# Hedgehog linear attention beside a gated MLP: query features turned by VectorE in 32-by-32 blocks instead of by TensorE, and the side work set from a table

## The chip, the cores and the metric

One core of one Trainium2 chip. The metric is the device time of one execution in microseconds: the median of the runs shown. The profile is one execution of the same program, with the hardware profiler on. PE is TensorE's matmul part and PEld its weight load, DVE is VectorE, ACT is ScalarE, POOL is GpSimd, SP is SyncE, which issues most DMAs.

## The reference

`x` is 2048 tokens by 640. It is normalised per token (`xn`), and two branches read it:

```python
qkv = (xn @ wqkv) -> q, k, v          # 32 heads of 20
pq = einsum("bhsd,hdf->bhsf", q, w_phi); pk = the same of k
phi_q = concat([softmax(pq), softmax(-pq)]); phi_k = the same of pk   # 40 features a head
kv = einsum("bhsf,bhsd->bhfd", phi_k, v);  z = sum of phi_k over s
num = phi_q @ kv;  den = phi_q @ z + 1e-6
s = (num / den) @ wo
g = silu(gelu(xn @ w1 + b1) @ w2 + b2)      # 640 -> 1536 -> 640
out = x + s * g
```

## The kernel before

All products are of 32-bit numbers. The large ones are split in a high and a low part (`split_w`, lines 134 to 140; hi by ScalarE, the rest by VectorE or GpSimd) and take three passes (`PASSES`, line 337).

**Phase 1** (0 to 238 us) projects keys, values and queries tile by tile of 128 tokens, sums the key-value state in PSUM, and stores the exponentials of each query tile, 128 tokens by 1280 features, in `e_dram`. The change does not touch it.

**The feed-forward units** (238 to 552 us) are 12: two halves of the tokens (1024 each, as two groups of 512), six groups of 256 hidden columns. A unit is seven groups of products (`part`, L1201, 54 products of 512 columns) and a down pass in two halves of 30 products (`down`, L1230), which VectorE adds to `ys` (L1239). Beside it run, called by hand at chosen points of the unit: loading and splitting `w1` and `w2`; and for each of 16 query tiles `q_load` (read back from `e_dram`) and `q_norm` (L1286 to L1305): GpSimd multiplies with the key sums (L1288), VectorE sums heads twice (L397), takes reciprocals (L1291, L1299) and three small products (L1295, L1298, L1301), GpSimd scales (L402), and SyncE stores the tile, token by token, in `phi_dram` (L1273).

**The tail** (from the last down pass on) works on four chunks of 512 tokens. A chunk's four tiles of `phi` are loaded. The products with `kv` need features on the partitions, so TensorE turns them: `num_t` (L1318 to L1328) makes four 128-by-120 transposes into a bank of PSUM (L1324) and ScalarE copies the bank to `ph` (L1327); 11 such steps per chunk. `num_m` then multiplies `ph` with the state `bdk` (120 features by 64 columns, L1335, 256 tokens at a time) or, for the last two heads, `bdl` (L1342); a 32-bit product shows as two instructions in the trace. ScalarE and VectorE split the result into `oT` (L1338, L1339) and `oTl` (L1347, L1348), and a DMA that ScalarE issues spreads rows of `oTl` into `oT` (`spread`). `finish` makes one output tile (five per chunk) of 15 products with `wo` (L1402), multiplies with the gate (L1404, two halves), adds the residual (L1405) and stores.

In `last_mid` and `num_groups`, the turning and the products of chunk 0 stand between the down products of the last unit, and those of the next chunk between the output tiles of the present one.

The order on each engine is the order in which the code emits instructions (`manual_schedule`); SyncE's queue too stands in that order. Tiles of SBUF come from pools (23 `slabs` of 5 KB a partition, 11 `rows`), PSUM has 8 banks in this part, and a new tile waits for the last reader of the one it replaces.

Of the kernel before, what the change touches and what calls it, by code (L numbers as in the profile page):

```python
# [40 lines left out]
def _ft(t):  # L41
    return (120 * t, 120 if t < 10 else 80)


@with_exitstack
def hedgehog_gated_mlp_kernel(ctx: ExitStack, tc: tile.TileContext, x, xt_in, wqk, bd, wv, wo, w1, b1, w2, b2, out_t):
# [47 lines left out]
    phi_dram = dram.tile([NT, P, 2 * D], F32, name="phi_dram")  # L94
# [491 lines left out]
    def w1_forms(raws):  # L586
# [632 lines left out]

    ys = [None] * KC  # L1220

    def down(g, ws, hs, o, mid=None):
        for ds in ((0, 1, 2), (3,), (4,)):
            pss = [bankB() for _ in ds]
            for i in range(GF):
                for d, ps in zip(ds, pss):
# [5 lines left out]
            for d, ps in zip(ds, pss):  # L1232
                if ys[d] is None:
                    ys[d] = slab(F32, f"y{d}", (P, 2, CW))
                y = ys[d][:, o, :]
                if g == 0:
                    nc.vector.tensor_copy(y, ps[:])
                else:
                    nc.vector.tensor_tensor(y, ps[:], y, op=OP.add)  # L1239
# [8 lines left out]
    def x_back(p):  # L1248
        hi, lo = slab(F32, "xhi", (P, 10, P)), slab(F32, "xlo", (P, 10, P))
        nc.sync.dma_start(hi[:], xp_dram[:, :, 0, at(p)])  # L1250
        nc.sync.dma_start(lo[:], xp_dram[:, :, 1, at(p)])
        return hi, lo

    def x_forms(p, hi, lo):
        nc.vector.tensor_tensor(hi[:], hi[:], lo[:], op=OP.add)
        yield
        tt = lo[:, :9]
        x_sums(lambda a, b: hi[:, a:b], lambda a, b: hi[:, a + 8:b + 8] if b <= 2 else hi[:, a + 3:b + 3], tt)
        yield
# [4 lines left out]
        nc.sync.dma_start(xd_dram[:, :, 1, at(p)], tt)


    stores, late_store = [], [False]

    def put(dst, src):
        if late_store[0]:  # L1270
            stores.append((dst, src))
        else:
            nc.sync.dma_start(dst, src)  # L1273

    def put_old(n):
        for _ in range(n):
            nc.sync.dma_start(*stores.pop(0))

    def q_load(t):
# [3 lines left out]
        return ef  # L1283

    def q_norm(t, ef):
        ez = slab(F32, "ez")  # L1286
        zv = ez[:].rearrange("p a b -> p (a b)")
        nc.gpsimd.tensor_tensor(zv, ef, zf, op=OP.mult)  # L1288
        yield
        rc = head_sums(ef, "rc")  # L1290
        nc.vector.reciprocal(rc[:], rc[:])  # L1291
# [26 lines left out]
    def num_t(phi, p, j):  # L1318
        ps = bankB()
        n = 120 if j < 5 else 80  # L1320
        for e in range(2):
            f, q = (2 * j + e, p) if j < 5 else (10, e)
            for i in range(2):
                nc.tensor.transpose(ps[:n, e * 256 + i * P:e * 256 + (i + 1) * P].bitcast(F32R),  # L1324
                                    phi[2 * q + i][:, 120 * f:120 * f + n], identr[:])
        ph = (row if (2 * j + p) % 2 else ph_tile)([P, 512], F32, "ph")
        nc.scalar.activation(ph[:n], ps[:n], AF.Copy)  # L1327
# [327 lines left out]
```

## Time and profile before

| | us |
|---|---|
| runs | 661.45, 661.48, 662.12; median 661.48 |
| profiled execution, its span | 659.8 |
| TensorE busy | 652.2 (99%), granted clock 1.00 |
| VectorE, ScalarE, GpSimd busy | 449.2, 325.4, 392.8 |
| DMA | 130.62 MB, mean 198 GB/s |
| transposes by TensorE (L1324), 176 | 542.6 to 626.1 |

The profile gives the span of its execution, from the first to the last instruction; it is 1.6 us under the median of the runs, which holds what lies around the span. A row of a group ends in busy time, mean ns of one, and idle time ahead of it with its releaser. A row of the chain is start, length and what.

### The profile page before, as it was taken

Reading aid. Unit: us, or ns where it says so; the run is one execution under the profiler, and the core shown is the slowest. Engines: PE = TensorE matmul, PEld = TensorE weight load, DVE = VectorE, ACT = ScalarE, POOL = GpSimd, SP = SyncE. Lnnn points to the kernel's source line nnn. Section 1 sums busy time; section 2 is a strip of 40 time slices with the busy share of each in tenths; the row PEclk is TensorE's granted clock in tenths of the full one; section 3 lists DMA queues with packets and bytes.
Section 4 is the critical chain, followed back from the end, with each engine's and each line's share of the span. In section 5 each row is a group of like instructions: output and inputs, shape, how many; then the busy total and the mean of one; then the engine's idle time right before and its main releaser. Section 6 shows DMA issues by size and latency. Waiting matters only on the chain.

```text
span 659.8 us, 11974 instructions
## 1 busy us (share of the span) xinstructions
PE 652.2 (99%) x4616; PEld 572.6 (87%) x4616; DVE 449.2 (68%) x714; ACT 325.4 (49%) x550; POOL 392.8 (60%) x344
## 2 busy tenths in 40 slices
PE   8999999999999999999999999999999999999997
PEld 8999999999999998888888888888888887877876
DVE  5878987766885756595885685777967877333132
ACT  4556777644666678435245138632132336645320
POOL 3597887774883437776875754746357665422322
PEclk9999999999999999999999999999999999999999
DMA  8436912031924882539656697456375275668444
GB/s 319 184 121 205 294 63 67 27 102 37 299 87 147 312 310 81 198 118 321 222 178 246 249 425 290 167 223 243 120 283 199 81 307 230 209 215 316 139 133 148
DMA packets 77081, 130.62 MB, mean 198 GB/s; under 512 B 5056, under 2 KB 44480, under 8 KB 76128
## 3 DMA queue, kind: packets, MB, share of 16 engines
q1 hardware_dynamic: 76704, 129.20, 55.0%
q10 hardware_dynamic: 320, 0.66, 0.6%
q8 instruction: 36, 0.59, 0.3%
q14 instruction: 21, 0.17, 0.1%
HBM read 81.66 MB, written 46.20 MB: 194 GB/s over the span
## 4 chain that ended last, share of the span: by engine, by line
PE 94%; POOL 2%; DMA 1%; issue 1%; DVE 1%; ACT 0%; SPq 0%; POOLq 0%
PE pB L1230 25%; PE pB L1201 22%; PE pW L485 20%; PE pB L1402 10%; PE pA L344 4%; PE pW L977 3%; PE pB L1335 3%; PE pB L1324 2%; PE pA L163 2%; PE kv L577 1%; DMA folds<-in_wqk_dram 1%; POOL tt L276 1%; POOL xd L295 0%; PE pB L1342 0%; PE pA L330 0%
## 5 line engine op out<-in xcount | busy, mean ns | idle before, releaser
L1230 PE MATMUL pB<-hs,w2s 128*128 128x512 f32 x720 | 167.0, 390 | 0.0
L1230 PEld LDWEIGHTS pB<-hs,w2s 128*128 128x128 f32 x720 | 134.6, 188 | 28.2 <-DVE oT L1339 0.4
L1201 PE MATMUL pB<-xp,w1s 128*128 128x512 f32 x324 | 81.3, 389 | 0.0
L1201 PE MATMUL pB<-xd,w1s 128*128 128x512 f32 x324 | 79.3, 389 | 0.0
L1239 DVE TENSOR_TENSOR y<-pB,y 128x512 f32<-128x512 f32 x100 | 63.7, 680 | 15.8 <-PE pB L1230 15.6
L1402 PE MATMUL pB<-oT,wo 128*128 128x512 f32 (+1 forms) x315 | 72.5, 385 | 0.2
L1201 PEld LDWEIGHTS pB<-xd,w1s 128*128 128x128 f32 x324 | 60.8, 188 | 12.6
L1201 PEld LDWEIGHTS pB<-xp,w1s 128*128 128x128 f32 x324 | 60.8, 188 | 12.6
L1206 ACT ACTIVATE pB<-pB,b1t 128x512 f32<-128x512 f32 x48 | 31.8, 662 | 77.6 <-DVE pB L1497 28.3
L1402 PEld LDWEIGHTS pB<-oT,wo 128*128 128x128 f32 x315 | 56.1, 188 | 13.0 <-DVE oT L1339 1.2
L402 POOL TENSOR_TENSOR eq<-eq,rc 128x1280 f32<-128x1280 f32 x16 | 37.9, 2369 | 48.7 <-DVE rc L1301 43.8
L383 POOL TENSOR_TENSOR e<-e,mxs 128x1280 f32<-128x1280 f32 x13 | 30.7, 2372 | 41.4 <-DVE mxs L378 25.7
L389 ACT ACTIVATE e<-e 128x1280 f32<-128x1280 f32 x32 | 40.8, 1274 | 17.9 <-POOL e L383 8.3
L601 POOL TENSOR_TENSOR w1s<-raw,w1s 128x640 fp32r<-128x640 f32 (+1 forms) x18 | 24.9, 1386 | 41.2 <-ACT w1s L600 41.1
L485 PE MATMUL pW<-wsum,xd 128*128 128x320 f32 x288 | 48.4, 310 | 0.0
L1288 POOL TENSOR_TENSOR ez<-eq,zrep 128x1280 f32<-128x1280 f32 x16 | 47.3, 2954 | 0.0
L1217 ACT ACTIVATE x<-pB 128x512 f32<-128x512 f32 x12 | 7.2, 600 | 78.9 <-PE pB L1201 78.9
L485 PEld LDWEIGHTS pW<-wsum,xd 128*128 128x128 f32 x288 | 43.6, 188 | 0.0
L138 POOL TENSOR_TENSOR w2s<-raw,w2s 128x640 fp32r<-128x640 f32 x24 | 37.1, 1567 | 7.1 <-ACT w2s L136 7.1
L402 POOL TENSOR_TENSOR e<-e,rc 128x1280 f32<-128x1280 f32 x15 | 36.1, 2410 | 5.8 <-DVE rc L838 4.2
L1327 ACT ACTIVATE ph<-pB 120x512 f32<-120x512 f32 (+1 forms) x44 | 22.9, 604 | 26.5 <-PE pB L1324 23.8
L1212 DVE TENSOR_TENSOR hs<-pB,hs 128x512 fp32r<-128x512 f32 x48 | 32.0, 685 | 5.2 <-ACT hs L1208 5.0
(216 smaller groups left out, 1282.1 us busy)
## 6 DMA issues: line engine op xcount, KB each, us to landing
raw<-in_w_dram SPq DMA_DIRECT2D x42, 320.0 KB
e_dram<-e SPq DMA_DIRECT2D x16, 640.0 KB
eq<-e_dram SPq DMA_DIRECT2D x16, 640.0 KB
phi_dram<-eq SPq DMA_DIRECT2D x16, 640.0 KB
phi<-phi_dram SPq DMA_DIRECT2D x16, 640.0 KB
xt<-in_x_dram SPq DMA_DIRECT2D x16, 320.0 KB
xres<-in_xt_dram SPq DMA_DIRECT2D x20, 256.0 KB
out_dram<-xres SPq DMA_DIRECT2D x18, 256.0 KB
```

The lines of the kernel that those rows point to most:

```text
L138: eng.tensor_tensor(sl[:, 1, :], raw, sl[:, 0, :].bitcast(F32), op=OP.subtract)
L383: eng.tensor_tensor(e3, e3, mx[:, :, None].to_broadcast([P, 64, DH]), op=OP.subtract)
L389: nc.scalar.activation(ef, ef, AF.Exp)
L402: eng.tensor_tensor(e3, e3, rc[:, :, None].to_broadcast([P, 64, DH]), op=OP.mult)
L485: nc.tensor.matmul(self.bank[ch][:, :HALF], self.x(blk, a), w(b), start=new and i == 0, stop=i == len(mms) - 1, skip_group_check=True)
L1201: nc.tensor.matmul(bank[ch][:], tl[:, a, off + wo_:off + wo_ + P], mov(blk, b), start=new and n == 0, stop=n == len(mms) - 1, skip_group_c ...
L1206: nc.scalar.activation(ps, ps, AF.Gelu_apprx_tanh, bias=b1t[:, f:f + 1])
L1212: nc.vector.tensor_tensor(hs[:, 1], ps, hs[:, 0].bitcast(F32), op=OP.subtract)
L1230: nc.tensor.matmul(ps[:], ws[i][:, b, d * P:(d + 1) * P], hs[o][i][:, a, :], start=i == n == 0, stop=(i, n) == (GF - 1, 2), skip_group_che ...
L1239: nc.vector.tensor_tensor(y, ps[:], y, op=OP.add)
L1288: nc.gpsimd.tensor_tensor(zv, ef, zf, op=OP.mult)
L1402: nc.tensor.matmul(ps[:, cols], w, o[:, a, cols], start=n == 0, stop=n == 14)
```

## The change

**The turning.** After scaling, VectorE turns each query tile in 32-by-32 blocks, in two halves of 640 features (`q_turn`), into a tile `pt` that holds two token tiles side by side. Four DMAs for each half of a pair, one per 32 partitions, store it feature by feature (`q_put2`): `phi_dram` is now by chunk, 1280 features by 512 tokens, and each run is 64 tokens (256 bytes). For the products, 120 features by 512 tokens (twice) or the last 80 are read straight into `ph`. `num_t`, its transposes and ScalarE's copies are gone. `num_m` multiplies 512 tokens at a time; the split to `oT` puts the tokens back in order (`by_token`).

**The table.** All side work of this part is set by numbers. `tick` counts places: 31 in each unit, then two in each output tile (one ahead of it, one after eight of its products); `when(place, f)` puts a step there. 372 is the place ahead of the first output tile.

```diff
+PLAN = {
+    "q": [
...
+        [351.75, 371.75, 372.55, 372.75, 373.75, 373.85, 374.75, 376.1],
+        [367.0, 374.25, 375.3, 375.5, 376.0, 376.6, 377.5, 377.6, 381.5, 378.6],
+        [370.25, 377.75, 378.55, 378.75, 379.75, 379.85, 380.75, 380.85],
+        [377, 381, 381.8, 382.5, 383, 383.1, 384, 384.1, 385, 385.1],
+    ],
...
+    "c_q": ["pool", "pool", "pool", "pool", "vector", "pool", "pool", "pool", "pool", "pool", "vector", "pool", "pool", "pool", "pool", "pool"],
...
-    phi_dram = dram.tile([NT, P, 2 * D], F32, name="phi_dram")
+    phi_dram = dram.tile([NCH, 2 * D, CW], F32, name="phi_dram")
...
+    def when(s, f, *args):
+        assert int(s) >= at_slot[0]
+        e = todo.setdefault(int(s), [])
+        e.append((s % 1, len(e), f, args))
+
+    def tick():
+        for _, _, f, args in sorted(todo.pop(at_slot[0], ()), key=lambda e: e[:2]):
+            f(*args)
+        at_slot[0] += 1
...
-        scale_heads(ef, rc)
-        yield
-        put(phi_dram[t], ef)
...
+    def q_scale(t):
+        scale_heads(qe[t][0], qe[t][2], ENG[PLAN["c_q"][t]])
+
+    def q_turn(t, h):
+        c, (u, v) = t // TPC, divmod(t % TPC, 2)
+        if v == 0:
+            pairs[c, u, h] = slab(F32, "pt", (P, 20, 2, 32))
+        nc.vector.transpose(pairs[c, u, h][:, :, v, :],
+                            qe[t][0][:, D * h:D * h + D].rearrange("p (b k) -> p b k", k=32))
+        if h:
+            qe.pop(t)
+
+    def q_put2(t, h):
+        c, u = t // TPC, t % TPC // 2
+        pt = pairs.pop((c, u, h))
+        dst = phi_dram[c, D * h:D * h + D].rearrange("(b i) n -> i b n", i=32)
+        for a in range(4):
+            nc.sync.dma_start(dst[:, :, P * a + 64 * u:P * a + 64 * u + 64],
+                              pt[32 * a:32 * a + 32].rearrange("p b t k -> p b (t k)"))
...
+    def load_phi_group(c, j):
+        if j == 5:
+            t = tail_row([P, CW], F32, "ph")
+            nc.sync.dma_start(t[:80], phi_dram[c, 1200:])
+        else:
+            t = slab(F32, "ph", (P, 2, CW))
+            nc.sync.dma_start(t[:120], phi_dram[c, 240 * j:240 * j + 240].rearrange("(e p) n -> p e n", p=120))
...
-            for i in range(2):
-                nc.tensor.transpose(ps[:n, e * 256 + i * P:e * 256 + (i + 1) * P].bitcast(F32R),
-                                    phi[2 * q + i][:, 120 * f:120 * f + n], identr[:])
-        ph = (row if (2 * j + p) % 2 else ph_tile)([P, 512], F32, "ph")
-        nc.scalar.activation(ph[:n], ps[:n], AF.Copy)
...
-                nc.tensor.matmul(po[64 * e:64 * e + 64, :256], bdk[:n, 2 * j + e, :], ph[:n, e * 256:(e + 1) * 256],
+                nc.tensor.matmul(po[64 * e:64 * e + 64, :], bdk[:120, 2 * j + e, :], ph[:120, e, :],
                                  start=True, stop=True)
...
+    def num_step(c):
...
+        j = nsteps[c].pop(0)
+        num_m(j, oTs[c], phis[c].pop(j))
+        if j < 5:
+            spread(j, oTs[c])
...
                 for n, (w, o, a) in enumerate(steps):
+                    if n == 8 and sl.start == 0:
+                        tick()
                     nc.tensor.matmul(ps[:, cols], w, o[:, a, cols], start=n == 0, stop=n == 14)
...
-            put(out_t[d * P:(d + 1) * P, c * CW:(c + 1) * CW], xr[:])
+            when(at_slot[0] + 2, nc.sync.dma_start, out_t[d * P:(d + 1) * P, c * CW:(c + 1) * CW], xr[:])
```

The eight numbers of a row of `q` are the places of load, product with the key sums, first head sum, second head sum, the four small steps, scaling and the two turns of one tile; a row of an odd tile ends with the places of the two stores. `c_q` names the engine that scales.

TensorE in the tail. Before, from the second half of the last unit's down pass (L1230) to the third output tile (L1402):

```order
L1230 MATMUL pB<-hs,w2s 128x512 x12
L1342 MATMUL pB<-ph,bdl 40x256 x2
L1335 MATMUL pB<-ph,bdk 64x256 x20
L1230 MATMUL pB<-hs,w2s 128x512 x12
L1402 MATMUL pB<-oT,wo 128x512 x15
L1324 MATMUL pB<-identr,phi 80x128 x4
L1324 MATMUL pB<-identr,phi 120x128 x12
L1402 MATMUL pB<-oT,wo 128x512 x15
L1324 MATMUL pB<-identr,phi 120x128 x16
L1402 MATMUL pB<-oT,wo 128x512 x15
```

And now (L1322 the down pass, L1459 and L1451 the feature products, L1519 the output tiles):

```order
L1459 MATMUL pB<-ph,bdl 40x256 x2
L1322 MATMUL pB<-hs,w2s 128x512 x3
L1451 MATMUL pB<-ph,bdk 64x512 x2
L1322 MATMUL pB<-hs,w2s 128x512 x3
L1451 MATMUL pB<-ph,bdk 64x512 x2
L1322 MATMUL pB<-hs,w2s 128x512 x12
L1451 MATMUL pB<-ph,bdk 64x512 x6
L1322 MATMUL pB<-hs,w2s 128x512 x12
L1519 MATMUL pB<-oT,wo 128x512 x8
L1459 MATMUL pB<-ph,bdl 40x256 x2
L1519 MATMUL pB<-oT,wo 128x512 x7
L1451 MATMUL pB<-ph,bdk 64x512 x2
```

The transposes are gone, and the feature products stand singly, between smaller groups of the others.

VectorE in the tail. Before, from the last addition of the down pass on (the second head sum and the small steps of the last query tile, then output tiles):

```order
L1239 TENSOR_TENSOR y_4736<-pB,y_4736 128x512
L397 TENSOR_REDUCE dn<-ez 128x64
L1295 TENSOR_TENSOR dn<-dn,rc 128x64
L1298 SCALAR_TENSOR_TENSOR den<-dn 128x32
L1299 RECIPROCAL den<-den 128x32
L1301 TENSOR_TENSOR rc<-rc,den 128x64
L1404 TENSOR_TENSOR y_4684<-pB,y_4684 128x256 x2
L1404 TENSOR_TENSOR y_4692<-pB,y_4692 128x256 x2
```

And now, from the fourth output tile on, with the turns of tile 14 and the sums of tile 15:

```order
L1521 TENSOR_TENSOR y_4760<-pB,y_4760 128x256 x2
L1409 STREAM_TRANSPOSE pt<-eq 128x20x32 x2
L475 TENSOR_REDUCE rc<-eq 128x64
L1386 RECIPROCAL rc<-rc 128x64
L1521 TENSOR_TENSOR y_4784<-pB,y_4784 128x256 x2
L475 TENSOR_REDUCE dn<-ez 128x64
L1394 TENSOR_TENSOR dn<-dn,rc 128x64
L1397 SCALAR_TENSOR_TENSOR den<-dn 128x32
L1398 RECIPROCAL den<-den 128x32
L1400 TENSOR_TENSOR rc<-rc,den 128x64
```

The norms of tiles 12 to 15 moved from the last two units to behind the last down addition, between the output tiles.

SyncE in the tail, from the stores of tile 13 to the loads of chunk 3. Now:

```order
L1419 DMA phi_dram<-pt 32x20x64 x4
L1492 DMA xres<-in_xt_dram 128x512
L1308 DMA out_dram<-xres 128x512 x2
L1492 DMA xres<-in_xt_dram 128x512
L1419 DMA phi_dram<-pt 32x20x64 x8
L1492 DMA xres<-in_xt_dram 128x512
L1308 DMA out_dram<-xres 128x512
L1435 DMA ph<-phi_dram 80x512
L1438 DMA ph<-phi_dram 120x2x512 x2
```

Before, the last stores of features and what followed:

```order
L1380 DMA xres<-in_xt_dram 128x512 x2
L1273 DMA phi_dram<-eq 128x1280 x2
L1380 DMA xres<-in_xt_dram 128x512
L1312 DMA phi<-phi_dram 128x1280 x2
L1380 DMA xres<-in_xt_dram 128x512
```

Two stores of whole tiles became sixteen of half pairs, and the last eight stand six output tiles later, right ahead of the loads that read them.

More of the change, by code (lines that the diff above doesn't have):

```diff
@@ L1263, in x_forms @@
         nc.sync.dma_start(xd_dram[:, :, 0, at(p)], hi[:, :9])
[L1264 to L1277, printed above, removed]
+        nc.sync.dma_start(xd_dram[:, :, 1, at(p)], lo[:, :9])
+        seen.add(("x", p))
+    qe = {}
@@ L1350, in spread @@
+                hi, lo = (by_token(oT[1][:40, b])[:, 2 * e:2 * e + 2] for b in range(2))
+                nc.scalar.activation(hi, src, AF.Copy)
+                nc.vector.tensor_tensor(lo, src, hi.bitcast(F32), op=OP.subtract)
     def spread(j, oT):
         nc.scalar.dma_start(oT[0][j][15::16].bitcast(F32), oT[1][8 * j:8 * j + 8].bitcast(F32))
[L1353 to L1367 removed]
+    def num_step(c):
+        if c not in oTs:
+            oTs[c] = new_oT(slabs if PLAN["c_oT"][c] == "slab" else late[0])
+            nsteps[c] = [5, 0, 1, 2, 3, 4]
+        j = nsteps[c].pop(0)
+        num_m(j, oTs[c], phis[c].pop(j))
+        if j < 5:
+            spread(j, oTs[c])
@@ L1513, in hedgehog_gated_mlp_kernel @@
                 q_sub(eb[o], 2 + o, nc.gpsimd)
-        next(xo, None)
-        silu(3)
-        hs = ((h11, h21), (None, h22))
-        if unit == NG - 1:
-            reload()
-        if unit == 0:
-            zf = kv_norm(kvr_out[0])
-        if not more:
-            phin = load_phi(ORDER[1])
+            zf_at.append(kv_norm(kvr_out[0]))
+        tick()
+        if last:
+            done[0] = True
+            seen.difference_update({("y", g, o, d) for o in range(2) for d in range(KC)})
@@ L1523, in hedgehog_gated_mlp_kernel @@
             xstack.close()
             ctx.enter_context(tc.tile_pool(name="pad", bufs=1)).tile([P, 32], F32, name="lpad")
-            late = ctx.enter_context(tc.tile_pool(name="late", bufs=10, reuse_waits="tile"))
-            tailp.append(ctx.enter_context(tc.tile_pool(name="phs", bufs=6)))
+            late.append(ctx.enter_context(tc.tile_pool(name="late", bufs=11, reuse_waits="tile")))
+            tailp.append(ctx.enter_context(tc.tile_pool(name="phs", bufs=3)))
             tailp.append(ctx.enter_context(tc.tile_pool(name="gts", bufs=3)))
-        w1f = w1_forms(w1r) if more and not back else none
@@ L1529, in hedgehog_gated_mlp_kernel @@
-        if back:
-            w1g = w1_back((unit + 1) % NG)
-        next(w1f, None)
-        if not more:
-            oT = new_oT(late)
-            groups = last_mid()
-        dn = down(g, w2g, hs, 0, None if more else delayed(groups, 4))
-        next(dn)
-        h12 = act_lo(*h12)
-        if unit == 0:
-            for o in range(2):
-                q_put(eb[o], 14 + o)
-        next(q1, None)
-        next(w1f, None)
-        next(dn)
-        next(w1f, None)
-        next(dn)
-        if not more:
-            next(dn)
-            next(dn)
-            break
@@ L1571, in hedgehog_gated_mlp_kernel @@
-        next(dn)
-        next(xg, None)
-        next(q2, None)
+        tick()
+        w2g = [w2_at.pop((unit, i)) for i in range(GF)]
+        hs = ((h11, h21), (None, h22))
+        for d, _ in enumerate(down(g, w2g, hs, 0)):
+            if d == 0:
+                h12 = act_lo(*h12)
+                if unit == 0:
+                    for o in range(2):
+                        q_put(eb[o], 14 + o)
+            if d == 3 and unit == NG:
+                kv_state(kvr_out[0])
+        hs = (None, (h12, h22))
@@ L1605, in hedgehog_gated_mlp_kernel @@
+            finish(c, d, oTs[c], ci == NCH - 1 and d >= 3)
+    for _ in range(3):
+        tick()
+    assert not todo
     ffn.close()
```

369 lines of the change are left out of this document (203 added, 166 removed), and 12 rows, old and new, of the table PLAN.

## The prediction

> **What bounds the kernel now.** First the page: busy times, the granted clock, and the chain of work that ended last.
>
> ```profile
> span 659.8 us, 11974 instructions
> PE 652.2 (99%) x4616; PEld 572.6 (87%) x4616; DVE 449.2 (68%) x714; ACT 325.4 (49%) x550; POOL 392.8 (60%) x344
> PEclk9999999999999999999999999999999999999999
> PE 94%; POOL 2%; DMA 1%; issue 1%; DVE 1%; ACT 0%; SPq 0%; POOLq 0%
> PE pB L1230 25%; PE pB L1201 22%; PE pW L485 20%; PE pB L1402 10%; PE pA L344 4%; PE pW L977 3%; PE pB L1335 3%; PE pB L1324 2%; PE pA L163 2%; PE kv L577 1%; DMA folds<-in_wqk_dram 1%; POOL tt L276 1%; POOL xd L295 0%; PE pB L1342 0%; PE pA L330 0%
> ```
>
> TensorE is busy 99% of the span at the full clock, and 94% of the chain is its work. A microsecond taken off TensorE is a microsecond of span as long as nothing else becomes late. So two questions: how much TensorE work goes, and what is late then.
>
> Next the chain in order of time, around the tail (start us, us, what):
>
> ```profile
> 537.50 5.44 PE pB L1230 x24
> 542.94 0.24 PE pB L1324 x4
> ...
> 544.62 1.26 PE pB L1324 x16
> ...
> 546.65 1.25 PE pB L1324 x16
> ...
> 548.67 0.61 PE pB L1324 x8
> ```
>
> and from the same view 12 us later:
>
> ```profile
> 552.10 0.56 PE pB L1342 x4
> 552.66 4.32 PE pB L1335 x40
> ...
> 558.62 0.40 DVE y L1239
> 559.02 1.96 DMA oT<-oTl
> 560.99 0.74 ACT wo L136
> ...
> 561.79 1.58 POOL wo L138
> ...
> 564.15 1.20 PE pB L1324 x16
> 565.35 3.52 PE pB L1402 x15
> 568.87 1.26 PE pB L1324 x16
> ...
> 573.64 0.93 PE pB L1324 x12
> ```
>
> L1324 is the turning by TensorE: 44 transposes per chunk of 512 tokens, always on the chain. Between 558.62 and 563.41 the chain leaves TensorE: a small lapse before the first output product. Last, how full the engines are by stretch; the columns are length, then busy time (instructions) of PE, PEld, DVE, ACT, POOL, then clock, DMA share, GB/s:
>
> ```profile
> 499.40:525.30 25.90, 25.90 (x116) 21.45 (x115) 20.27 (x32) 9.15 (x15) 21.50 (x14) 1.00 0.39 147
> 565.30:590.00 24.70, 24.70 (x150) 19.25 (x150) 7.30 (x20) 12.46 (x28) 8.65 (x11) 1.00 0.73 253
> 590.00:616.00 26.00, 26.00 (x168) 20.57 (x167) 8.07 (x23) 10.96 (x25) 7.14 (x10) 1.00 0.72 240
> ```
>
> The first row is a feed-forward unit: TensorE has no gap in it, and VectorE some 5 us of 26 free. In the tail VectorE has 17 of 25 free.
>
> **The turning goes.** Chunk 0: 0.24 + 1.26 + 1.25 + 0.61 = 3.36 us. Chunk 1: 1.20 + 1.26 + 0.93 = 3.39 us. Chunks 2 and 3 have the same 44 instructions and the same counts; at 3.39 each the sum is 13.5 us, the 2% that the chain gives L1324. All 176 lie on the chain, so 13.5 us leave it. The 44 copies out of PSUM on ScalarE (L1327) go too; ScalarE is half idle, and that is worth nothing by itself.
>
> **The feature products** (L1335) become 80 instructions of 512 columns instead of 160 of 256. Now 40 take 4.32 us, 108 ns each, so two take 216 ns. A 512-column product of the down pass takes 5.44 / 24 = 227 ns. So the cost is 80 x (0 to 11 ns) = 0 to +0.9 us; I take +0.4.
>
> **The lapse.** From 552.10 to 564.15 are 12.05 us. In it TensorE's own work is 0.56 + 4.32, then 12 down products (12 x 0.227 = 2.72) and the 15 products of the first output tile (3.52): 11.12. So 0.9 us is lost there. In the changed order the feature products of chunk 0 stand one by one between the down products, and each tile of weights `wo` is split before: I take all 0.9 off, with 0 as the other end.
>
> Dense, that gives 13.5 + 0.9 - 0.4 = 14.0 us less.
>
> **What becomes late: the last four query tiles.** Before, tiles 14 and 15 had their sums while the last unit ran. Now tiles 12 to 15 are normalised, turned and stored in the tail, after the last down pass. Chunk 3 is made of just these four, and TensorE stands in order: the first product of chunk 3 (the 40-column one after the eight products of output tile 10) blocks everything behind it. I work out when TensorE gets there and when the data does. The rows (mean ns of one is the last figure before the second bar):
>
> ```profile
> L1288 POOL TENSOR_TENSOR ez<-eq,zrep 128x1280 f32<-128x1280 f32 x16 | 47.3, 2954 | 0.0
> L402 POOL TENSOR_TENSOR eq<-eq,rc 128x1280 f32<-128x1280 f32 x16 | 37.9, 2369 | 48.7 <-DVE rc L1301 43.8 <-issue 4.9
> L397 DVE TENSOR_REDUCE rc<-eq 128x64 f32<-128x1280 f32 x16 | 23.6, 1476 | 0.0
> L1291 DVE RECIPROCAL rc<-rc 128x64 f32<-128x64 f32 x16 | 8.9, 553 | 0.6
> L1295 DVE TENSOR_TENSOR dn<-dn,rc 128x64 f32<-128x64 f32 x16 | 8.8, 551 | 0.0
> L1298 DVE SCALAR_TENSOR_TENSOR den<-dn 128x32 f32<-128x32 f32 x16 | 7.3, 459 | 0.5
> L1299 DVE RECIPROCAL den<-den 128x32 f32<-128x32 f32 x16 | 5.7, 353 | 0.5
> L1301 DVE TENSOR_TENSOR rc<-rc,den 128x64 f32<-128x64 f32 x16 | 3.6, 225 | 0.6
> L1237 DVE COPY y<-pB 128x512 f32<-128x512 f32 x20 | 13.2, 685 | 5.1 <-PE pB L1230 5.1
> L1348 DVE TENSOR_TENSOR oTl<-pB,oTl 40x256 fp32r<-40x256 f32 x8 | 3.4, 421 | 2.6 <-ACT oTl L1347 2.6
> ```
>
> The trace has no 32-by-32 transpose. It reads and writes 640 numbers a partition; the copy of 512 takes 0.685 us and the reduction of 1280 takes 1.476. Between these ends I take 0.78, as 640 is nearer to 512. Two more rows of the timeline show that instructions back to back cost less than their means:
>
> ```profile
> 522.74 1.82 DVE L1239 TENSOR_TENSOR y<-pB,y 128x512 f32<-128x512 f32 x3
> ...
> 641.93 0.76 DVE L1404 TENSOR_TENSOR gt<-pB,gt 128x256 f32<-128x256 f32 x2 [2.64 <-issue]
> ```
>
> So 0.61 us for a 512-column one, 0.76 for the two halves of an output tile. VectorE's queue from the last down addition to the second turn of tile 15, counted in the order: 8 reductions (11.8), 4 reciprocals (2.2), 4 times the four small steps (4 x 1.59 = 6.4), 8 turns (6.2), 4 `oTl` parts (1.7), 7 `oT` parts (4.3), 6 output tiles (4.6): 37.2 us. TensorE in that time, from the end of the down pass T: 158 output products at 3.52 / 15 = 0.235 (37.1) and the features of chunks 1 and 2 (2 x 4.88 = 9.8): it arrives at T + 46.9.
>
> After the turns comes the store. Its row, the nearest there is, is a store of 512-byte packets:
>
> ```profile
> DMA packets 2083, 1.05 MB, mean 175 GB/s; under 512 B 32, under 2 KB 2083, under 8 KB 2083
> q1 hardware_dynamic: 2083, 1.05, 58.0%
> xd_dram<-xlo SPq DMA_DIRECT2D x1, 576.0 KB
> ```
>
> That answer is for 310 to 316 us: 0.58 x 6 us x 16 engines / 2083 = 26.7 ns a packet of 512 bytes. The new store has packets of 256 bytes, 2560 for a half tile pair, 160 an engine: at half a packet's time 2.1 us, at the whole 4.3; I take 3.2 (20 ns). With some 2 us to land (the `oT` row above, 1.96), 0.4 to issue each way, and the load of 160 KB and its landing (2.5), chunk 3 is ready 8.5 us after the turns: T + 0.7 + 37.2 + 8.5 = T + 46.4, if VectorE never waits. That is just in time. But it does wait. The scaling by GpSimd (2.37) needs the four small steps, and the turn right behind needs the scaling; between them stand one output tile and an `oT` part (0.76 + 0.61). So about 1.0 us is lost per tile, 4 us in all, and the arrival of chunk 3 is at T + 50.4: a new stall of 3.5 us. Its ends are 0 and, with the longer turn (8 x 0.7 = 5.6) and the longer packet (1.1), 10.
>
> Forecast: the profiled span 659.8 - 14.0 + 3.5 = 649.3. The median of the runs, 661.5, lies 1.7 above that span, so 651.0.
>
> **Other edits with one answer.** In the units the side work is now set at 31 places per unit, one query tile a unit: VectorE gets 2 turns (1.6 us) where the row above has 5 us free, and loses the second tile of the late units (two reductions, a reciprocal and the four steps, 5.1 us). Low parts moved between GpSimd and VectorE lie beside TensorE. SyncE now waits for a turn ahead of each store, and the loads of weights queue behind it. In the table they stand 10 places (of 25.9 / 31 = 0.84 us) or more ahead of their use, and the wait is short, since the store stands behind its turn: nothing. In the tail, residuals, gates and `ph` queue behind the store of tile 15; all are for output tile 10 and later, so what they cost is in the sum. Even before, SyncE stood 13 us at a store in the tail, and nothing came late:
>
> ```profile
> 554.20 12.98 SPq L1273 DMA_DIRECT2D phi_dram<-eq  x2
> ```
>
> **A rule against the change.** The row gives 26.7 ns for a 512-byte store packet; nothing in this trace stores less. The Trainium skill, DMA: Bandwidth & Descriptors, Specifications, says that line rate needs at least 512 B, and that below this the engine does a read-modify-write. By that rule 256 bytes would cost no less than 512, and a read added to the write could double it. With the whole packet time of the row (4.3 instead of 3.2 us) the sum is 652.1; what double would do is worked out as the third rival.
>
> **Rivals.**
>
> *No new stall.* VectorE's small steps (0.55 and 0.46 on average, 0.2 for the like-sized last one) may be quick when GpSimd is idle; that is 4 x 0.6 = 2.4 us less, and with packets at half the row's time 1.1 less: T + 46.9, in time. 661.5 - 14.0 = 647.5. Chance 0.22.
>
> *VectorE becomes the bound of the tail.* If it falls back, PSUM banks come free late and TensorE also waits in chunk 2's features; stalls of 7 to 12 us, 654.5 to 659.5. For it: 37.2 us of VectorE work in 47. Chance 0.16.
>
> *Slower: the stores.* The stores of tiles 13 and 15 are 640 packets an engine, starting near T + 21, with 8 us of other transfers among them. At p ns a packet they end at T + 29 + 0.64p, and 4 us later the data is there. The whole gain is gone when the stall is 14, at T + 61: p = 44 ns. At twice the row, 53 ns, it is T + 67, a stall of 20 and 667.5 us. Against it: the 512-byte stores of the row move 175 / 0.58 = 302 GB/s, and the tail at 565 to 590, with rows of 2 KB and more, 253 / 0.73 = 347, so shorter packets have so far cost 15%. Chance 0.12. (The rule of the Trainium skill above would lead here, and no run yet shows it.)
>
> *It does nothing measurable*, the stalls eating all but 1.3 us: 0.04.
>
> **The numbers.** The forecast, stalls of 1.5 to 6.5 us (649 to 654), has 0.46. The range 646.5 to 659.0 holds it, the dense case and nearly all of the third: some 0.83. A measurement here tells 0.2%, 1.3 us, from no change. Faster 0.84, same 0.04, slower 0.12.
>
> **What would show it.** Right: no transposes on TensorE; in the tail TensorE idle once, 2 to 6 us, ahead of chunk 3's first product, released by the load of `ph`; VectorE busy over 34 of the 47 us after the last down pass; turns of 0.7 to 0.85 us; store packets of 13 to 27 ns. Wrong: gaps between units 1 and 11; turns over 1 us; stalls at chunk 2; packets over 40 ns.

## The result and the profile after

The changed kernel takes 667.49 us (median of 4 runs, 666.20 to 668.42); the kernel before, beside it on the same chip, 661.77. The ratio is 1.0088, with a 95% interval of 1.0073 to 1.0102: slower, where 651.0 was forecast, and above the top of the range (659.0).

The page of the changed kernel, busy times and chain:

```profile
span 666.4 us, 11468 instructions
PE 647.2 (97%) x4360; PEld 550.6 (83%) x4360; DVE 468.2 (70%) x731; ACT 304.0 (46%) x488; POOL 387.5 (58%) x339
PEclk9999999999999999999999999999999999999799
PE 77%; DMA 7%; POOL 5%; DVE 4%; ACT 3%; issue 2%; SPq 1%; ACTq 0%; POOLq 0%; DVEq 0%
```

TensorE works 5 us less than before (652.2), but the span is 6.6 us longer. A quarter of the chain is now outside TensorE, where it was 6%, and in one slice near the end the granted clock is down. What TensorE waited for, of the list of waits (us in total, times, longest):

```profile
PE pB L1519 <- DMA oT<-oTl: 8.4, 6, 4.3
PE pB L1459 <- DMA ph<-phi_dram: 1.4, 1, 1.4
...
PE pB L1280 <- POOL w1s L679: 0.9, 1, 0.9
```

The stall that the prediction was about, the wait of chunk 3's first product for `ph`, is there with 1.4 us. The big one stands above it: the output products (L1519) wait six times for the spread, the small DMA that puts rows of `oTl` into `oT`. To see where the 6.6 us lie, one needs the starts of units 0, 2 and 11, and of the output products. Before (timeline of TensorE; below it the row of the output products: count, ns of one, first and last start):

```profile
238.25 1.55 PE L1201 MATMUL pB<-xp,w1s 128*128 128x512 f32 x6
...
292.15 1.52 PE L1201 MATMUL pB<-xp,w1s 128*128 128x512 f32 x6
...
525.10 1.52 PE L1201 MATMUL pB<-xp,w1s 128*128 128x512 f32 x6
L1402 PE MATMUL pB<-oT,wo x315: 278/389/504, 559.8 to 655.3; 128*128 128x512 f32 x143, 128*128 128x256 f32 x15
```

and after:

```profile
239.02 1.55 PE L1280 MATMUL pB<-xp,w1s 128*128 128x512 f32 x6
...
295.19 1.52 PE L1280 MATMUL pB<-xp,w1s 128*128 128x512 f32 x6
...
528.27 1.52 PE L1280 MATMUL pB<-xp,w1s 128*128 128x512 f32 x6
L1519 PE MATMUL pB<-oT,wo x315: 278/389/765, 560.3 to 662.2; 128*128 128x512 f32 x143, 128*128 128x256 f32 x15
```

| stretch | before | after | difference |
|---|---|---|---|
| up to unit 0 | 238.25 | 239.02 | +0.8 |
| units 0 and 1 | 53.90 | 56.17 | +2.3 |
| units 2 to 10 | 232.95 | 233.08 | +0.1 |
| unit 11 to the first output product (turning and features of chunk 0 in it) | 34.7 | 32.0 | -2.7 |
| first to last output product (chunks 1 to 3 in it) | 95.5 | 101.9 | +6.4 |
| rest | 4.5 | 4.2 | -0.3 |

The first row differs as much between executions of one and the same code (237.8 to 239.0 in the runs below) and is not pursued. So three things are to be explained: 2.3 us in units 0 and 1, and a tail that is 6.4 us longer although 10.2 us of turning (three chunks at 3.39) have left it.

The tail, after, in the timeline of TensorE: chunk 2's last features, then output tile 10, where chunk 3's first features stand.

```profile
605.52 1.08 PE L1451 MATMUL pB<-ph,bdk 120*64 120x512 f32 x4
606.53 8.95 PE L1519 MATMUL pB<-oT,wo 128*128 128x512 f32 x38
616.85 0.63 PE L1459 MATMUL pB<-ph,bdl 80*40 80x256 f32 x4 [1.37 <-DMA ph<-phi_dram]
...
622.95 1.62 PE L1519 MATMUL pB<-oT,wo 128*128 128x512 f32 x3 [4.34 <-DMA oT<-oTl]
624.49 1.98 PE L1451 MATMUL pB<-ph,bdk 120*64 120x512 f32 x4
```

The spread of chunk 2 lands 4.34 us late. And the four feature products behind it take 1.98 us instead of 1.08: the clock. Two-microsecond stretches (length, then busy time and instructions of PE, PEld, DVE, ACT, POOL; the third from the end is the granted clock):

```profile
620.00:622.00 2.00, 0.00 (x0) 0.00 (x0) 0.00 (x0) 0.00 (x0) 0.00 (x0) 0.50 1.03 254
622.00:624.00 2.00, 1.05 (x3) 0.83 (x3) 0.00 (x0) 0.00 (x0) 0.00 (x0) 0.50 1.04 250
624.00:626.00 2.00, 2.00 (x6) 0.30 (x4) 0.76 (x2) 0.00 (x0) 0.90 (x2) 0.50 1.02 334
```

The granted clock falls to 0.50 within the stall and stays there until about 626.4, when TensorE has been at work again for 3.4 us. By an estimate, half of these 3.4 us is lost as well, so that the wait of 4.34 us costs about 6.

Why the spread was late, in the timeline of ScalarE:

```profile
593.73 0.38 ACT L1464 ACTIVATE oTl<-pB 40x256 fp32r<-40x256 f32 x1 [3.42 <-DMA phi_dram<-pt]
602.38 0.38 ACT L1464 ACTIVATE oTl<-pB 40x256 fp32r<-40x256 f32 x1 [8.27 <-DVE oTl L1465]
...
615.06 0.57 ACTq L1468 DMA_DIRECT2D oT<-oTl  x1
```

and of VectorE, which ScalarE waited for at 602.38:

```profile
595.03 1.57 DVE L1409 STREAM_TRANSPOSE pt<-eq 128x640 f32<-128x640 f32 x2 [1.87 <-POOL eq L480]
596.53 1.44 DVE L475 TENSOR_REDUCE rc<-eq 128x64 f32<-128x1280 f32 x1
...
599.34 1.49 DVE L475 TENSOR_REDUCE dn<-ez 128x64 f32<-128x1280 f32 x1 [0.17 <-POOL ez L1381]
...
601.93 0.41 DVE L1465 TENSOR_TENSOR oTl<-pB,oTl 40x256 fp32r<-40x256 f32 x1
...
607.80 0.83 DVE L1409 STREAM_TRANSPOSE pt<-eq 128x640 f32<-128x640 f32 x1
```

The low part of `oTl` (L1465) is half a microsecond of work and stands behind turns and sums of tiles 14 and 15. The prediction counted this queue as what makes chunk 3 late; it also carries the low parts that chunks 1 and 2 need, and those are due sooner. The way of the spread comes on top: the last one is issued at 615.06, and TensorE goes on only at 622.95, while the DMA share is 1.02 to 1.04 in the stretches above.

### The profile page after: what moved, and what is told of

It is laid out like the page before. It is cut to its first block, busy times and chain, and to the rows that moved or that the text cites. A ratio compares the mean times of both kernels' runs of the same rounds, so it can differ in the third digit from the quotient of the medians.

```text
span 666.4 us, 11468 instructions
## 1 busy us (share of the span) xinstructions
PE 647.2 (97%) x4360; PEld 550.6 (83%) x4360; DVE 468.2 (70%) x731; ACT 304.0 (46%) x488; POOL 387.5 (58%) x339
## 4 chain that ended last, share of the span: by engine, by line
PE 77%; DMA 7%; POOL 5%; DVE 4%; ACT 3%; issue 2%; SPq 1%; ACTq 0%; POOLq 0%; DVEq 0%
PE pB L1322 22%; PE pB L1280 20%; PE pW L563 19%; PE pB L1519 5%; PE pA L422 4%; PE pW L1056 3%; DMA xres<-in_xt_dram 2%; PE pA L241 2%; PE kv L655 1%; DMA eq<-e_dram 1%; DMA phi_dram<-pt 1%; DMA oT<-oTl 1%; PE pB L1451 1%; POOL e L461 1%; POOL ez L1381 1%
## 5 line engine op out<-in xcount | busy, mean ns | idle before, releaser
L1322 PE MATMUL pB<-hs,w2s 128*128 128x512 f32 x720 | 166.7, 390 | 0.4 <-DVE hs L1291 0.4
L1322 PEld LDWEIGHTS pB<-hs,w2s 128*128 128x128 f32 x720 | 134.7, 188 | 31.3 <-issue 2.8
L1519 PEld LDWEIGHTS pB<-oT,wo 128*128 128x128 f32 x315 | 55.9, 189 | 34.3 <-issue 20.1
L1519 PE MATMUL pB<-oT,wo 128*128 128x512 f32 (+1 forms) x315 | 75.9, 391 | 8.4 <-DMA oT<-oTl 8.4
L480 POOL TENSOR_TENSOR eq<-eq,rc 128x1280 f32<-128x1280 f32 x14 | 33.2, 2370 | 65.7 <-DVE rc L1400 61.5
L216 POOL TENSOR_TENSOR w2s<-raw,w2s 128x640 fp32r<-128x640 f32 x23 | 35.7, 1575 | 34.6 <-ACT w2s L214 34.6
L1409 DVE STREAM_TRANSPOSE pt<-eq 128x640 f32<-128x640 f32 x32 | 26.0, 828 | 13.6 <-POOL eq L480 13.6
L679 POOL TENSOR_TENSOR w1s<-raw,w1s 128x384 fp32r<-128x384 f32 (+1 forms) x15 | 19.6, 1307 | 25.1 <-ACT w1s L678 25.1
```

Of the source, the lines that this page charges most:

```text
L216: eng.tensor_tensor(sl[:, 1, :], raw, sl[:, 0, :].bitcast(F32), op=OP.subtract)
L480: eng.tensor_tensor(e3, e3, rc[:, :, None].to_broadcast([P, 64, DH]), op=OP.mult)
L1322: nc.tensor.matmul(ps[:], ws[i][:, b, d * P:(d + 1) * P], hs[o][i][:, a, :], start=i == n == 0, stop=(i, n) == (GF - 1, 2), skip_group_che ...
L1519: nc.tensor.matmul(ps[:, cols], w, o[:, a, cols], start=n == 0, stop=n == 14)
```

## The experiments

Theories: **Q**, the queue of VectorE and GpSimd in the tail, as just shown. **L**, lanes: in the program, the transfers that SyncE and ScalarE issue take eight semaphores in turn, and each waits until the one eight issues earlier has landed. Rows of the order of ScalarE and of SyncE, with what each waits for:

```
L1468 DMA oT<-oTl 8x1024 [waits DMAHW6_49,DVE_49]
L1468 DMA oT<-oTl 8x1024 [waits DMAHW1_49,DVE_49]
...
L1492 DMA xres<-in_xt_dram 128x512 [waits DMAHW3_49]
L1308 DMA out_dram<-xres 128x512 [waits DMAHW4_49,Pool_49]
...
L1419 DMA phi_dram<-pt 32x20x64 [waits DMAHW5_49]
```

With 64 small stores instead of 16, ScalarE can stand at a spread until some load of SyncE has landed. **S**, the 256-byte packets themselves; **D**, full DMA engines, which make the spread itself slow; **F**, tile 0 on GpSimd in units 0 and 1; **W**, the price of going back and forth between feature and output products; **C**, crowding in the units.

**1. The last four tiles' sums left out.**

```diff
-            when(k, f, *[b for b in a if b is not None])
+            if t < 12 or f in (q_load, q_turn):
+                when(k, f, *[b for b in a if b is not None])
```

> Leaves out, for tiles 12 to 15 alone, the two sums, the reciprocal, the four small steps, the product with z and the scaling, so that chunk 3's features are not normalised; the loads, turns, stores and everything after them stay. Theory Q (the queue of VectorE and GpSimd in the tail makes the low parts of oT late, so the spread of the last rows lands late and TensorE waits in output tiles 0, 5 and 10): VectorE loses 4 x (2 x 1.48 + 0.55 + 1.59) = 20 us in the tail, the waits of L1519 on oT go from 8.4 us to under 2, the time falls from 667.5 to 654 to 658. Theory S (the 64 stores of 256-byte packets crowd the DMA engines) and theory L (64 stores instead of 16 make the few DMA lanes wait for each other, and ScalarE with them): these stay as they are, so 664 or more and the waits on oT over 5 us.

Measured: 661.09 us, ratio to before 0.999 (0.998 to 0.9999). Faster than the changed kernel by 6.4, but not by the 9.5 or more that Q alone gave; one wait of 4.4 us was left, and half clock behind it. ScalarE in this run:

```profile
576.44 0.57 ACTq L1468 DMA_DIRECT2D oT<-oTl  x1
577.06 0.72 ACT L1505 ACTIVATE y<-y,b2t 128x512 f32<-128x512 f32 x1 [6.72 <-DMA ph<-phi_dram]
...
586.91 0.57 ACTq L1468 DMA_DIRECT2D oT<-oTl  x1
587.52 1.34 ACT L1505 ACTIVATE y<-y,b2t 128x512 f32<-128x512 f32 x2 [4.70 <-DMA out_dram<-xres]
```

VectorE was now free, and ScalarE still stood 6.72 us at one spread and 4.70 at another, until a load of `ph` and a store of the output had landed, with which the spread has nothing to do but the lane. Q is half of the story; L is the other candidate.

**2. and 3. Long packets, and one store instead of four.** The bytes go to wrong places of the intermediate. The first two added lines are kernel 2 (`dst` is a view in eight contiguous pieces), the last is kernel 3 (in two).

```diff
-        for a in range(4):
-            nc.sync.dma_start(dst[:, :, P * a + 64 * u:P * a + 64 * u + 64], ...)
+        for a in range(4):
+            nc.sync.dma_start(dst[4 * u + a], pt[32 * a:32 * a + 32].rearrange("p b t k -> p (b t k)"))
+        nc.sync.dma_start(dst[u], pt[:].rearrange("p b t k -> p (b t k)"))
```

> The same 64 stores of the same bytes, but each partition writes its 5120 bytes in one piece, so the numbers land in the wrong places of the intermediate and the features are of mixed-up data. Theory S: the share of the DMA engines in the tail falls by a third or more and the time falls by 6 us or more, to 661 or less. Theories Q and L: the number of stores and all waits between engines stay, so within 2 us of 667.5.

> As the kernel with long pieces (wrong places, the same bytes), but one store a half tile pair instead of four: 16 stores instead of 64. Theory L: 3 us or more below the kernel with 64 long stores, and the idle time of ScalarE that ends with unrelated transfers (3.4 to 3.8 us each) gone. Theory Q: within 1.5 us of the kernel with 64 long stores, since the low parts are as late as before.

Measured: 671.56 (1.0154, 1.0129 to 1.0179) and 672.38 us (1.0160, 1.0145 to 1.0176): both some 4 to 5 us slower than the changed kernel, which no theory said. Packets from 545 to 625 us, changed kernel, then 2:

```profile
DMA packets 22338, 17.90 MB, mean 224 GB/s; under 512 B 16426, under 2 KB 16426, under 8 KB 22334
```

```profile
DMA packets 7943, 18.29 MB, mean 229 GB/s; under 512 B 1072, under 2 KB 1072, under 8 KB 7939
```

The short packets are gone and the engines move as much as before. The waits on `oT` are 10.9 and 9.9 us, and TensorE is at half clock for 17.1 us in 2 and 13.7 us in 3, where the changed kernel has 6.8. S is refuted. With Q in place, fewer stores do not help either. The longer time at half clock goes with the slower result; why the stalls fell so differently stays open.

**4. Tile 0's product behind w1's low parts.** On GpSimd, at the end of unit 0, the product of tile 0 (2.96) stands ahead of the low part of `w1` that TensorE waits for at the start of unit 1 (changed kernel):

```profile
264.68 2.96 POOL L1381 TENSOR_TENSOR ez<-eq,zrep 128x1280 f32<-128x1280 f32 x1
267.60 1.54 POOL L679 TENSOR_TENSOR w1s<-raw,w1s 128x640 fp32r<-128x640 f32 x1
```

```diff
-        [1.7, 11.5, 14, 22, 23, 24, 30, 30],
+        [1.7, 17.5, 19, 24, 25, 25.5, 33, 34],
```

> Tile 0's side work alone moves within units 0 and 1: the product with z from place 11.5 to 17.5, behind the four low parts of w1 on GpSimd, its first sum from 14 to 19, the rest 1 to 4 places later, the two turns no longer next to each other. Theory F (the 3.0 us that units 0 and 1 lost are the wait for w1's low part behind that product, 0.9, and the lapses around it): unit 11 begins 1 to 2.5 us earlier than at 528.4, and the time falls by as much. Rival (they come from the end of the stage before or from work in general being denser): within 0.7 us of 667.5.

Measured: 672.00 us (1.0159, 1.0137 to 1.0182). The wait for `w1s` is gone, and a worse one is there; VectorE:

```profile
272.66 1.49 DVE L475 TENSOR_REDUCE dn<-ez 128x64 f32<-128x1280 f32 x1 [8.15 <-POOL ez L1381]
```

It stood 8.15 us at the second sum, ahead of the additions that free PSUM, and TensorE waited 3.9 us for one of them. A refuted edit, not a refuted theory.

**5. and 6. All tiles within the units; tile 0's second sum later too.** Kernel 5, tiles 8 and 15 (those between every 17.5 places); kernel 6 is 4 with `[1.7, 17.5, 19, 40, 42, 43, 52, 53]` for tile 0.

```diff
-        [238.75, 253, 261, 263.5, 267, 267.1, 274, 275],
+        [228.0, 235.0, 237.0, 241.0, 242.5, 242.6, 246.5, 247.5],
...
-        [377, 381, 381.8, 382.5, 383, 383.1, 384, 384.1, 385, 385.1],
+        [350.5, 357.5, 359.5, 363.5, 365.0, 365.1, 369.0, 370.0, 370.5, 370.6],
```

> Tiles 8 to 15 each in 20 places instead of 36 to 50, one every 17.5 places from 228 on, so that tile 15 is turned at place 370 and nothing of tiles 12 to 15 lies in the tail; the low parts of w1 for unit 11 and the scaling of tile 10 go from VectorE to GpSimd to make room. Nothing else changes. Theory Q (tail queue of the last four tiles): the waits on oT fall under 2.5 us, TensorE's clock stays at 1.00 in the tail, and the tail loses at most 4 us more than its own work; with the 2.4 us of units 0 and 1 still lost the time is 651 to 656. Theory L (the lanes of the 64 stores and of the loads): the stores leave the tail as well, so the same; told apart by the two kernels without the sums. Rival (VectorE in the units is full with 1.8 tiles a unit, 6.7 us each on 10 us of other work in 25.9): TensorE waits between units 7 and 11, the time is 660 or more.

> As the kernel with tile 0's product behind w1's low parts, but its second sum and all that follows 16 to 20 places later, behind the end of that product on GpSimd, so that VectorE no longer stands before it. Theory F: units 0 and 1 together take 53.8 to 54.8 us instead of 56.2 and the time falls by 1 to 2.4 us from 667.5, if the tail stays as it is. Rival: what was lost there comes back at another wait (the turns ahead of unit 2's additions), 56 us or more. The tail's stalls may move the total by some us either way, as in the last runs, so the units' starts are the measure.

Measured: 668.14 (1.0095, 1.0079 to 1.0111) and 672.75 us (1.0173, 1.0146 to 1.0200). In 5, the units held: from unit 7's start to unit 11's it took 103.9 us, before 103.4, so VectorE was not full. One instruction of VectorE undid it:

```profile
558.50 1.49 DVE L475 TENSOR_REDUCE rc<-eq 128x64 f32<-128x1280 f32 x1 [8.37 <-DMA eq<-e_dram]
```

Tile 15's first sum stood 8.37 us for its load, with `y`'s addition and chunk 0's `oTl` behind it; TensorE lost 5.4 us to a bank, and then half clock. In 6, units 0 and 1 took 54.6 us, as F said, but the low part of w1 came 3.8 us late one unit on: the wait had moved, as its rival said.

**7. and 8. Without the sums (as 1), and the lanes relieved.** In 7 one store for four, in 8 the spreads from GpSimd.

```diff
-        nc.scalar.dma_start(oT[0][j][15::16]...
+        nc.gpsimd.dma_start(oT[0][j][15::16]...   (8)
```

> Leaves out the sums, small steps, products and scaling of tiles 12 to 15 (as the kernel at 661.1 us), and also writes each half tile pair by one store in long pieces (wrong places) instead of four. Theory L: with fewer stores the spread's issue no longer waits for unrelated transfers; the remaining wait of 4.4 us on oT and the 3.3 us at half clock behind it go, so 652 to 655. Theory D (the spread is issued in time and its small packets land late because the DMA engines are full with loads): the stall stays, 658 to 662.

> Leaves out the same work of tiles 12 to 15, keeps the 64 stores, and issues the spreads from GpSimd's DMA queue instead of ScalarE's. Theory L: GpSimd's transfers have lanes of their own and ScalarE is not held, so the stall of 4.4 us and its half clock go: 652 to 656. Theory D: the spread lands as late as before, 659 to 662.

Measured: 658.89 us (656.38 to 662.11; 0.9959, 0.9939 to 0.9979) and 654.95 us (0.9901, 0.9886 to 0.9916). In 8 the list of waits has no row for `oT` and the output products take 88.9 us:

```profile
L1519 PE MATMUL pB<-oT,wo x315: 277/389/504, 559.8 to 648.7; 128*128 128x512 f32 x143, 128*128 128x256 f32 x15
```

GpSimd issues the same spread that stood 6.72 us in run 1 as soon as VectorE has the low part:

```profile
569.94 0.53 POOL L1468 DMA_DIRECT2D oT<-oTl  x1 [2.52 <-DVE oT L1456]
```

and the DMA engines are as full as they can be, without harm:

```profile
560.00:590.00 30.00, 30.00 (x126) 17.80 (x125) 16.57 (x32) 9.38 (x17) 9.82 (x15) 1.00 0.98 270
```

The spreads are no faster on their way either (from 550 to 640 us; the last figure is the median from issue to landing):

```profile
oT<-oTl POOLq DMA_DIRECT2D x20, 32.0 KB, 4.9
```

L is shown, and D alone is refuted: between 1 and 8 only the issuing engine differs, and with it the lanes, and what went is the wait ahead of the issue. Full engines do make the way long (from 2.1 to 7.4 us in 8), which costs nothing where the issue is early and is part of the stall where it is late, as at 615.06 in the changed kernel. 7 lies between, and its runs scatter: fewer stores relieve the lanes in part.

**9, 10, 11. Kernels that do all the work.** 9 is the changed kernel with the spreads from GpSimd. 10 has no tile in unit 0: tiles 0 to 6 at the places of 1 to 7, tiles 7 to 15 every 16 places from 228. 11 is 10 with the spreads from GpSimd.

> One word changed: the spreads of the last rows are issued from GpSimd's queue instead of ScalarE's; all work of the changed kernel stays. Theory Q+L (two causes in a row: the low parts are late because VectorE and GpSimd are filled with tiles 12 to 15, and ScalarE is held at the spread's issue by the shared lanes): the lanes' part goes, the low parts stay late, and GpSimd now stands at the spreads with the scaling of a tile behind it: 658 to 665, waits on oT down from 8.4 to 2 to 6 us. Theory L alone: as the kernel without the sums and with this change, 655 or less.

> No tile in unit 0: tiles 0 to 6 take the places of tiles 1 to 7, tiles 7 to 15 follow every 16 places from 228 on in 20 places each, with the loads of tiles 14 and 15 at places 335 and 338; low parts of w1 for unit 11 on GpSimd. The spreads stay on ScalarE. Theory F: units 0 and 1 take 53.8 to 54.5 us together instead of 56.2. Theory Q: no wait of over 3 us at half clock in the tail; the lanes' waits of ScalarE may remain. 651 to 657. Rival (VectorE full in units 7 to 11 with 1.9 tiles a unit, or another row of its queue that stands ahead of its data): over 659.

> The same shifted order, and the spreads from GpSimd's queue. All three theories (F, Q, L) together say that only the dense tail is left: 13.5 us of turning less and 2 to 3 us for the wider feature products more than before, 649 to 653, with TensorE never idle over 1 us in the tail. If it is over 656, one of them is wrong or there is a fourth cause.

Measured: 662.45 (1.0010, 0.9996 to 1.0024), 663.41 (1.0023, 1.0007 to 1.0039), 664.30 us (1.0032, 1.0018 to 1.0045). 9 is as Q+L said: 5 us come from the one word, and what is left is Q, in 9's list of waits now with the stall that was forecast:

```profile
PE pB L1459 <- DMA ph<-phi_dram: 3.3, 1, 3.3
PE pB L1519 <- DMA oT<-oTl: 2.7, 3, 1.6
```

10 bears F out, at the edge of its range. Units 0 and 1 take 54.5 us:

```profile
238.19 1.55 PE L1280 MATMUL pB<-xp,w1s 128*128 128x512 f32 x6
...
292.69 1.52 PE L1280 MATMUL pB<-xp,w1s 128*128 128x512 f32 x6
```

But 10 and 11 lost at the seam between the last unit and the tail instead, in the first output tile, with tile 15's sums beside chunk 0's features (waits on `oT` of 3.9 and 3.7 us), and 3.8 us from the start of unit 6 to that of unit 11. 11 is over 656, which by its own expectation says that there is another cause: the seam, the later units, and W below.

**12, 13, 14. The features in groups.** 12 is kernel 8 with each of chunks 1 to 3 in two groups of three feature steps. 13 does all work: tiles 0 to 6 as in 10, tiles 7 to 14 every 16 places from 224 with the second sum 8.5 places behind the product, tile 15 alone in the tail, spreads from GpSimd, chunk 0's features 2 to 3 places earlier. 14 is 13 with the groups:

```diff
-        [373, 374, 375, 376, 377, 378],
+        [374, 374, 374, 377, 377, 377],
```

> As the kernel at 654.95 us (sums, small steps, products and scaling of tiles 12 to 15 left out, spreads from GpSimd), but the six feature steps of chunks 1, 2 and 3 stand in two groups of three instead of one by one between the output products. Theory W (each change between feature and output products costs TensorE 0.25 to 0.3 us: 0.09 ahead, 0.05 to 0.1 in the first pair and 0.11 behind): 3 to 4 changes fewer in each of three chunks, so 2.3 to 3.6 us less, 651.3 to 652.7. Rival (the price lies in the 512-column product itself, or grouping makes TensorE wait for PSUM banks, since VectorE and ScalarE take 1.3 us of one group's bank after another): 654 to 657.

> All work kept. Tiles 0 to 6 at the places of tiles 1 to 7; tiles 7 to 14 every 16 places from 224 on, each in 23 places so that no second sum stands on VectorE before its product is done; tile 15 alone in the tail, ahead of output tile 5; chunk 0's features 2 to 3 places earlier; spreads from GpSimd. Theories F, Q and L together: units 0 and 1 54.5 us, the later units 25.9 each, tail waits under 2 us: 650 to 655. If VectorE is full in the units (rival): starts of units 7 to 11 more than 0.5 us late each, 656 to 662.

> As the mixed order, with the features of chunks 1, 2 and 3 in two groups of three. Theory W: 2.3 to 3.6 us below the mixed kernel. Rival: the spreads come later by up to two places, and TensorE waits for them at output tiles 5, 10 or 15: no gain.

Measured: 656.86 (0.9922, 0.9905 to 0.9939), 660.18 (0.9979, 0.9969 to 0.9988) and 655.84 us (0.9920, 0.9895 to 0.9945). In 12 TensorE now came to `ph` before its load had (2.8 and 0.8 us of waits), and nothing was gained: the rival's number, for a reason that it did not name. Its output products take 88.9 us as in 8, with these 3.6 us of waits in them. In the other pair there are no such waits; output products of 13 and of 14:

```profile
L1519 PE MATMUL pB<-oT,wo x315: 278/389/504, 563.0 to 652.3; 128*128 128x512 f32 x143, 128*128 128x256 f32 x15
```

```profile
L1519 PE MATMUL pB<-oT,wo x315: 277/389/504, 564.3 to 649.0; 128*128 128x512 f32 x143, 128*128 128x256 f32 x15
```

89.3 against 84.7 us: 4.6 us in three chunks, a little above W's 2.3 to 3.6, are the price of standing one by one. These are eleven changes fewer, so some 0.4 us for each. In 14 twelve feature products in a row take 2.73 us, 228 ns each, while four alone took 1.01 (606.53 - 605.52 above), 253 ns:

```profile
575.62 2.79 PE L1451 MATMUL pB<-ph,bdk 120*64 120x512 f32 x12
578.35 3.03 PE L1519 MATMUL pB<-oT,wo 128*128 128x512 f32 x12
```

The output products beside them pay as well: in 8, eight that stand between two single steps take 2.06 us from start to start, 258 ns each, where the kernel before needs 235. 14 is faster than both kernels.

**15. Evenly spaced.** Tiles 6 to 14 every 16.5 places from 205, the rest as in 14.

> As the mixed and grouped kernel, but tile 6 too is done in 23 places, and tiles 6 to 14 follow every 16.5 places from 205 on, so that no two tiles' sums fall in the same half unit; from unit 6's start to unit 11's the mixed kernel took 133.7 us, the kernel before 129.6. Theory C (the 4.1 us come from two tiles' sums and turns next to each other ahead of the additions that free PSUM banks, at 459 to 461 above all): 131.5 or less, and the time 652.5 to 655. Rival (VectorE is simply full with 1.9 tiles a unit, wherever they stand): 133 us or more, and no gain over 655.8.

Measured: 654.69 us (653.93 to 658.93; 0.9905, 0.9888 to 0.9922), not told apart from 14. Start of unit 6 and of unit 11:

```profile
396.16 1.61 PE L1280 MATMUL pB<-xp,w1s 128*128 128x512 f32 x6 [0.23 <-DMA xp<-xp_dram]
...
528.79 1.52 PE L1280 MATMUL pB<-xp,w1s 128*128 128x512 f32 x6
```

132.6 us lie between the two forecasts (131.5 or less, 133 or more); whether the 3 us over the kernel before are crowding or a full VectorE was not settled.

## Why the prediction was wrong

**The dense sum was right, for another order than the one in the diff.** Of the 14.0 us, the output stretch was to lose three turnings (10.2) and the lapse (0.9) and to gain 0.3: from 95.5 to 84.7. Kernel 14 has 84.7. The turning is gone, as was said, and it is worth what was said. (In 14 other places lost: units 2 to 10 take 237.4 us there, 4.4 more than before.)

The changed kernel's span is 17.1 us above the forecast 649.3. Of these, 9.1 are stalls in the output stretch (12.6 where 3.5 were counted), 4.6 feature products, 2.3 units 0 and 1, and 1.1 are left for the rest. The steps that failed, one by one:

**The feature products: the step that took +0.4 for four chunks.** It priced the instruction (216 to 227 ns for 512 columns) and not its place. In a row that is right (228). But before they stood 40 in a row, and now by fours between output products; that costs 4.6 us in three chunks, against two groups a chunk (runs 13 and 14). The step on the lapse noted that they stand one by one, and booked it as a gain.

**The stall: the step that took 3.5 us at chunk 3.** The work that it counted is there: the turn took 828 ns for 780, and VectorE was busy 37.9 us in the 46.9 us after the down pass, where 37.2 were counted; rows of the changed kernel:

```profile
L1409 DVE STREAM_TRANSPOSE pt<-eq 128x640 f32<-128x640 f32 x32 | 26.0, 828 | 13.6 <-POOL eq L480 13.6
...
560.50:607.40 46.90, 42.80 (x172) 24.18 (x172) 37.87 (x65) 12.99 (x22) 29.06 (x20) 1.00 0.81 218
```

Its dates are not. VectorE stood idle 9 us in that stretch, and the last turn ended 48.1 us after the down pass (607.80 + 0.83 - 560.5), where 41.9 were reckoned (0.7 + 37.2 + 4). From there to the first product of chunk 3 (616.85) are 8.2 us, where 8.5 were counted; that this comes out is no proof of its parts, of which no row shows the 2.5 for the load. TensorE came to that product 55 us after the down pass and not 46.9, because it had been held up before. So the stall at chunk 3 was 1.4 us, less than forecast, with both dates some 6 to 8 us late.

What failed is the question asked of that queue: only when its last row is done. Its other rows, the low parts, have a date too, at output tiles 0, 5 and 10. With them 12.6 us were lost in the output stretch (101.9 - 84.7 - 4.6): 9.8 in waits, the rest mostly at half clock behind the long one. Two causes carry it: the work of tiles 12 to 15 (run 1 takes 6.4 us off) and ScalarE held at the lanes (run 9 takes 5.0 off, run 8 another 6.1 after run 1). The prediction had nothing of the second. That the change made it costly by having four times as many stores is likely and only partly shown: with a fourth of them, run 7 is 2.2 us below run 1, and run 3 not below run 2.

**The edits that cost nothing.** Units 2 to 10 took 0.1 us more, nothing, as was said. Units 0 and 1 did not: GpSimd had no room for tile 0 there, 2.3 us, 1.7 of which goes with tile 0 (run 10: 54.5 for 56.2, before 53.9). The prediction looked at VectorE's free time in a late unit and not at GpSimd's in the first two.

**The rivals.** The second (VectorE the bound of the tail) had the right engine and stalls near the right size (9.8 us of waits, for 7 to 12) at another wait: no PSUM bank was late, the low parts were. The third hit the number, 667.5, by luck: it rests on stores of 53 ns a packet and is refuted. The trace, in a stretch of almost nothing but such stores (605.5 to 611 us):

```profile
DMA packets 3608, 0.96 MB, mean 175 GB/s; under 512 B 3592, under 2 KB 3592, under 8 KB 3608
...
q1 hardware_dynamic: 3576, 0.90, 66.3%
```

0.663 x 5.5 us x 16 / 3576 = 16.3 ns a packet, within the 13.4 to 26.7 of the forecast. The Trainium skill, DMA: Bandwidth & Descriptors, Specifications, says that below 512 B the engine does a read-modify-write. Whether it does one here cannot be seen; the 256-byte store packet costs less time in this trace than the 26.7 ns of the 512-byte one, not more, and the measurement decides.

## What to carry to other kernels

When work is moved into a queue, ask of every row that stands behind it when it is due, not only of the last one. A DMA that waits for a semaphore shared with other transfers holds the whole engine that issues it, so small urgent transfers belong on a queue with few others. And a change that is right by its sum can still be slower by its order: the same work took 667.5 us as it was placed and 655 us in another placing, with the spreads and a few low parts on another engine (runs 14 and 15).

## What the runs showed of the hardware

- After waits of TensorE of 4.34 us (changed kernel), 3.9 (run 10) and 3.0 (run 15) the granted clock was 0.50 for a stretch that reached into the work behind, 6.8 us long in the changed kernel and 3.4 in run 10. The length of one wait does not decide it: in run 11 the clock stayed at 1.00 after a wait of 2.4 us, and in run 6 it fell after one of 1.9, with waits of 1.2 and 0.2 us shortly before. The Trainium skill, TensorE: Matmul & The Clock Gate, Part 1, says that the clock goes to half after an idle window of about 3.4 us, of a window that runs free. The 3.4 and 6.8 us at half clock are one and two such windows; that waits shorter than the window bring it about, as here, is not in that sentence, and the measurement decides.
- Going from output to feature products and back costs TensorE time, though no engine is waited for: five or six such turns a chunk instead of two cost about 1.5 us a chunk (runs 13 and 14).
- With the DMA engines 98% busy (run 8) a spread took from 2.1 to 7.4 us from issue to landing, and no stall came of it, since it was issued in time.
